# A spectral block and an MLP with all gradients on one core: w1 in column groups, the two MLP weight gradients placed earlier, the last product interleaved with the modulation gradients

## The chip, the core and the metric

The kernel runs on one core of a Trainium2 chip. The metric is the time on the device for one execution, in microseconds, smaller being better. A core has TensorE (PE in the profile, its weight loads PEld), VectorE (DVE), ScalarE (ACT), GpSimd (POOL) and SyncE (SP). Transfers between DRAM and on-chip memory are issued from SP's queue and from POOL's queue; the 16 DMA engines of the core carry both.

## The reference

The forward pass, on x of 2048 tokens by 1024 features in bfloat16, is

```
sa, ca, ga, sb, cb, gb = silu(c) @ w_mod           # six rows of 1024
h = layernorm(x) * (1 + ca) + sa
x = x + ga * irfft2(rfft2(h) * (w_r + 1j * w_i))   # spectral part, A
h = layernorm(x) * (1 + cb) + sb
y = layernorm(h)
x = x + gb * (gelu(y @ w1 + b1) @ w2 + b2)         # MLP, B; hidden width 3584
```

The kernel returns this x and the gradients for A_x, w_r, w_i, w1 (out_4), b1, w2 (out_6), b2, c and w_mod (out_9), given a gradient for the output. B_x is a constant and is not used.

## The kernel before

The program is written as one long sequence on one core. A scheduler of the language orders the instructions of each engine at build time, by the order of the program, the dependences and the memory slots that are free; what it writes down is then fixed, and each engine and each queue runs its list in order, waiting on semaphores. On-chip memory is cut into named regions (tags such as `px0` to `px5`, `sma`, `smb`, `t0` to `t3`, `uv0` to `uv3`, `fr`, `ot`, `wt`, `ph`, `gm`, `sb`): a tile with the tag of an earlier one can be written only when everything that reads the earlier one is done. PSUM has eight banks of 128x512 float32: two with tag `s`, two with `d`, four with `f`. A product of 128x128 by 128x512 is one matmul instruction.

The stages, in the order of the program:

- Modulation rows, matrices of the transforms, the gradient times gb (d_gBo), layernorm and folding of x (lines 169 to 540).
- The spectral forward (`spectral_core`, L342): products with the token transform (`s_fwd`, pu, L337), eight pairs (`pair`: products pcs, L360; complex multiplication with w_r and w_i on DVE, the weights gathered by POOL), products pv (L420), and for each quarter of the tokens products po (L455) and a `consume` function.
- The gradient through w2: `pp` (L575), 896 products, stored to d_ph. It is scheduled into the gaps of the spectral forward.
- The MLP forward with the gradient through the gelu (L601 to L670). `z_block` multiplies one of seven groups of 512 hidden features at a time (32 products pz, L614), then works on ACT and DVE, and stores the hidden values to d_hh and the gradient to d_gz. `bo_pass` multiplies by w2, 112 products pbo (L649) for half of the output columns of a quarter of the tokens, with w2 loaded in seven pieces through three buffers (L645). w1 stays on chip in eight tiles, one for 128 rows each, all 3584 columns wide (L584).
- The MLP backward (L690 to L754): w1 loaded again, transposed, in seven tiles w1T (L696), 896 products pg (L722), then two layernorm gradients (`ln_bwd`) on DVE and ACT, with column sums accS and accC, and the folding into fbuf2.
- The spectral backward, the same `spectral_core` with `consume_bwd` (L773): column sums accCA, `ln_bwd` and out_1. Its o4 tile `ct` has one buffer for the four quarters.
- gw2, the gradient for w2 (L803 to L822): 896 products over 28 row tiles fc. The hidden values come back transposed from d_hh in pieces of 256 features (L812, two buffers), gBo in four tiles gB (L806); the sums are copied by ACT (L821) and stored by POOL to out_6 (L822).
- Column sums accGA, and the gradient for w_mod (L851 to L864): 48 pieces, each loaded (wrw, L860) and reduced by DVE (L863), and made by ACT (gww, L861) and stored by POOL (L862), with four buffers each. "w_mod" in the text is this loop.
- gw1, the gradient for w1 (L876 to L896): 896 products in seven blocks, the gradient transposed from d_gz in 2 MB pieces (L885, two buffers), the sums copied by ACT (L893) and DVE (L895) in turn and stored by POOL (L896).

Though gw2 and gw1 stand at the end of the program, gw2 is started by the scheduler in the gaps of the last quarter products, since its d_hh buffers and gB tiles use memory that is free by then.

## Time and profile before

Three runs took 1913.84, 1921.5 and 1923.69 us; the median is 1921.5. The profiled execution took 1915.37 us, of which its span is 1913.6.

| engine | busy, us | share of the span |
|---|---|---|
| TensorE | 1514.3 | 79% |
| VectorE | 991.2 | 52% |
| ScalarE | 826.9 | 43% |
| GpSimd | 353.2 | 18% |

The two DMA queues moved 347.87 MB, 182 GB/s on the mean. The chain of work that ended last is, by line, issue of instructions (8.8%), the gw2 products (5.8%) and the gw1 products (3.4%), with the rest in many small pieces. A busy share over 1913.6 us is a mean over stages that are bound by different things, so the stages are read one at a time: the busy time of each engine in a stretch, the granted TensorE clock there, the share of time in which the DMA engines were busy (the records overlap a little, so a share can be somewhat over 1), and the waits by who ended them.

### The profile page before, as it was taken

To read this page: it belongs to the slowest core of one execution; us is meant where nothing else is said; L and a number is where in the kernel's file an instruction comes from. 1 tells how busy PE (TensorE), PEld (TensorE's weight loads), DVE (VectorE), ACT (ScalarE), POOL (GpSimd) and SP (SyncE) were. 2 spreads that over 40 slices of the span, in tenths; PEclk is the share of its full clock that TensorE was granted. 3 is DMA by queue.
4 is the path that set the end of the run, shared out by engine and by line. 5 is a ranking of instruction groups with operands and counts; after the bars stand their busy time and mean duration, and the time that the engine had idled before them with its cause. 6 is when DMAs were issued, how large, how long until landed. Compare 5 with 4: busy or idle time off the path is not lost. (4 is left out here: it accounts for less than half of the span.)

```text
span 1913.6 us, 18102 instructions
## 1 busy us (share of the span) xinstructions
PE 1514.3 (79%) x6590; PEld 681.7 (36%) x6722; DVE 991.2 (52%) x1380; ACT 826.9 (43%) x1097; POOL 353.2 (18%) x422
## 2 busy tenths in 40 slices
PE   2328998778988999998688999295479998817998
PEld 1103544333433343443233444042234443303443
DVE  1535556652288667677203787837556660464110
ACT  4636556775566555565011433253333341362000
POOL 5631331111111111111000001015201011132111
PEclk8659998889999999999899999598789999958999
DMA  9994485694365576657993444424636678698551
GB/s 336 254 274 124 125 253 179 175 259 119 111 187 202 198 225 205 203 160 215 202 271 103 165 154 177 131 66 133 176 105 163 160 231 205 214 326 201 125 127 36
DMA packets 396115, 347.87 MB, mean 182 GB/s; under 512 B 245997, under 2 KB 332013, under 8 KB 395898
## 3 DMA queue, kind: packets, MB, share of 16 engines
q1 hardware_dynamic: 361242, 228.17, 45.8%
q0 software_dynamic: 34784, 118.55, 17.8%
q8 instruction: 52, 0.85, 0.2%
q14 instruction: 37, 0.30, 0.0%
HBM read 168.34 MB, written 120.65 MB: 151 GB/s over the span
## 5 line engine op out<-in xcount | busy, mean ns | idle before, releaser
L889 PE MATMUL gw1acc<-gzs,n3n 128*128 128x512 bf16 x879 | 197.1, 385 | 62.1 <-ACT gwo L893 44.6
L575 PE MATMUL pp<-gBoT,wt 128*128 128x512 bf16 x875 | 202.5, 387 | 15.9 <-ACT phr L577 14.8
L722 PE MATMUL pg<-w1T,gzr 128*128 128x512 bf16 x879 | 198.9, 383 | 10.3 <-ACT gn3a L726 5.2
L889 PEld LDWEIGHTS <-n3n 128*128 128x128 bf16 x896 | 88.5, 99 | 170.3 <-issue 67.1
L157 DVE TENSOR_TENSOR ct<-ct 128x2048 bf16<-128x2048 bf16 (+1 forms) x76 | 103.4, 1389 | 60.4 <-ACT ct L457 40.5
L575 PEld LDWEIGHTS <-wt 128*128 128x128 bf16 x896 | 89.7, 100 | 121.9 <-issue 22.2
L614 PEld LDWEIGHTS <-w 128*128 128x128 bf16 x896 | 87.0, 98 | 122.7 <-issue 20.1
L722 PEld LDWEIGHTS <-gzr 128*128 128x128 bf16 x896 | 88.0, 98 | 118.2 <-issue 10.3
L649 PEld LDWEIGHTS <-hhA 128*128 128x128 bf16 x704 | 70.7, 101 | 126.1 <-issue 48.6
L157 DVE TENSOR_TENSOR gt<-gt,gt 128x2048 bf16<-128x2048 bf16 x84 | 102.1, 1224 | 17.9 <-ACT gt L621 17.0
L819 PE MATMUL gw2acc<-gB,hhsA 128*128 128x512 bf16 x438 | 103.3, 393 | 6.1 <-DMA hhsA<-d_hh 5.6
L614 PE MATMUL pz<-n3Tb,w 128*128 128x512 bf16 x439 | 100.3, 381 | 8.1 <-ACT gt L616 7.6
L614 PE MATMUL pz<-n3Ta,w 128*128 128x512 bf16 x438 | 99.2, 379 | 6.1 <-ACT gt L616 5.7
L577 ACT CAST phr<-pp 128x512 bf16<-128x512 f32 x112 | 62.8, 586 | 92.6 <-PE pp L575 58.6
L819 PE MATMUL gw2acc<-gB,otl 128*128 128x512 bf16 x439 | 100.9, 386 | 0.6 <-issue 0.2
L616 ACT ACTIVATE gt<-pz,b_col 128x512 bf16<-128x512 f32 x112 | 74.6, 682 | 50.8 <-PE pz L614 49.5
L895 DVE CAST gwo<-gw1acc 128x512 bf16<-128x512 f32 x28 | 19.3, 691 | 148.6 <-PE gw1acc L889 142.4
L420 PE MATMUL pv<-smi,R 128*128 128x512 bf16 x248 | 60.8, 391 | 40.3 <-DVE R L157 38.1
L893 ACT CAST gwo<-gw1acc 128x512 bf16<-128x512 f32 x28 | 16.3, 584 | 157.1 <-PE gw1acc L889 140.7
L821 ACT CAST gwo<-gw2acc 128x512 bf16<-128x512 f32 x56 | 32.7, 583 | 114.3 <-PE gw2acc L819 106.2
L455 PE MATMUL po<-gm,V 128*128 128x256 bf16 x256 | 45.2, 325 | 45.0 <-ACT ct L457 44.7
L578 POOL DMA_DIRECT2D d_ph<-phr x56 | 40.1, 716 | 210.9 <-ACT phr L577 183.0
(237 smaller groups left out, 2507.5 us busy)
## 6 DMA issues: line engine op xcount, KB each, us to landing
d_ph<-phr POOLq DMA_DIRECT2D x56, 256.0 KB, 3.6
d_gz<-gt POOLq DMA_DIRECT2D x28, 512.0 KB, 5.2
gzr<-d_gz SPq DMA_DIRECT2D x28, 512.0 KB, 7.5
wrw<-in_w_mod_dram SPq DMA_DIRECT2D x48, 256.0 KB, 3.8
out_dram<-gww POOLq DMA_DIRECT2D x48, 256.0 KB, 4.7
d_hh<-hhA POOLq DMA_DIRECT2D x22, 512.0 KB, 4.7
w2sA<-in_B_w_dram SPq DMA_DIRECT2D x19, 512.0 KB, 6.1
w2sB<-in_B_w_dram SPq DMA_DIRECT2D x19, 512.0 KB, 6.2
```

The lines of the kernel that those rows point to most:

```text
L157: nc.vector.tensor_tensor(out=out, in0=a, in1=b, op=op)
L420: nc.tensor.matmul(pv[:], lhsT=R[:, cl * 4 + m, :, :].rearrange("p x w -> p (x w)")[:, base:base + 255:2], rhs=smi[:, cl // 2, m, :], star ...
L455: nc.tensor.matmul(po[:, d2 * 256:(d2 + 1) * 256], lhsT=Vs[cl][:, 2 * dc + h, i * P:(i + 1) * P], rhs=gm[:, gi, :], start=(h == 0), stop=( ...
L575: nc.tensor.matmul(pp[:], lhsT=w2t[:, cch, k * P:(k + 1) * P], rhs=gBoT[b][:, cch, :], start=(cch == 0), stop=(cch == NDC - 1))
L577: nc.scalar.copy(out=ph2[:, k, :], in_=pp[:])
L578: nc.gpsimd.dma_start(out=d_ph_v[:, 2 * fg:2 * fg + 2, b * BW:(b + 1) * BW], in_=ph2)
L614: nc.tensor.matmul(pz[:], lhsT=w1s[cch][:, fc * P:(fc + 1) * P], rhs=n3T[:, cch, :], start=(cch == 0), stop=(cch == NDC - 1))
L616: nc.scalar.activation(out=zb[:, k, :], in_=pz[:], func=ACT.Identity, bias=b1_col[:, fc:fc + 1], scale=1.0)
L649: nc.tensor.matmul(pbs[i][:], lhsT=hh[:, k, i * P:(i + 1) * P], rhs=wp[:, k, :], start=False, stop=(g == 6 and k == 3))
L722: nc.tensor.matmul(pgs[i][:], lhsT=gzt[g][:, k, i * P:(i + 1) * P], rhs=w1Ts[g][:, k, h * KH:(h + 1) * KH], start=(g == 0 and k == 0), sto ...
L819: nc.tensor.matmul(acc[:], lhsT=hhs[:, t, k * P:(k + 1) * P], rhs=gBs[t // 4][:, t % 4, h * KH:(h + 1) * KH], start=(t == 0), stop=(t == N ...
L889: nc.tensor.matmul(acc[:], lhsT=n3ns[t // 4][:, t % 4, cch * P:(cch + 1) * P], rhs=gzs[:, t, :], start=(t == 0), stop=(t == NT - 1))
```

## The change

Five things change.

1. w1 is kept in seven tiles of 512 columns (a group g) by all 1024 rows, loaded one after the other. `z_block` for group g reads tile g alone, so a tile is free for w1T_g as soon as the last quarter's group g is multiplied; w1 and w1T use the same list of tags.
2. The region `px1` is no longer part of w1. Half of it is a fourth buffer for w2, half holds a row of sums `gacc`. The output passes add their column sums there through a PSUM bank each (pa), in place of two banks held throughout (accG); the freed banks (tag `d`) take every second pz.
3. The gB loads, and buffers for d_hh, are placed ahead of the spectral backward in the program. d_hh is now loaded in 28 pieces of 128 features with two buffers in `px1`, which is free at the end of the MLP forward, and two in `ot`. The tile empf moves to `wt`. The banks of accCA are taken, and set to zero by two products with a zero tile, before the spectral backward starts.
4. The last two row tiles of gw2 are summed at once in four banks, one quarter of the tokens after the other.
5. gw1 is split into `gw1_block`s. Block 0 follows gw2; one further block stands behind each of the six rows of w_mod. d_gz is loaded in halves (8 of 16 token tiles) with four buffers.

```
-    W1T = ["sma", "smb"] + PXT
+    W1T = PXT[2:6] + ["sma", "smb", "px0"]
...
-    for cch in range(NDC):
-        wtile = reg.tile([P, F], BF16, name=f"w1_{cch}", tag=W1T[cch])
-        nc.sync.dma_start(out=wtile[:], in_=w1_v[:, cch, :])
+    for g in range(7):
+        wtile = reg.tile([P, NDC, BW], BF16, name=f"w1_{g}", tag=W1T[g])
+        nc.sync.dma_start(out=wtile[:], in_=w1_v[:, :, g * BW:(g + 1) * BW])
...
+    px1t = reg.tile([P, 2, 4, BW], BF16, name="w2sD", tag="px1")
...
+    gacc = px1t[0:1, 1].rearrange("p a b -> p (a b)").bitcast(FP32)
...
-                pz = ps_s("pz")
+                pz = (ps_s, ps_d)[k % 2]("pz")
...
-            wp = w2p[w2n[0] % 3]
+            wp = w2p[w2n[0] % 4]
...
-            nc.tensor.matmul(accG[h][:], lhsT=ones_bf[:], rhs=go[:, i, :], start=(b == 0 and i == 0), stop=(b == 3 and i == 3))
+            nc.tensor.matmul(pa[:], lhsT=ones_bf[:], rhs=go[:, i, :], start=(i == 0), stop=(i == 3))
+        if b == 0:
+            nc.vector.tensor_copy(out=gacc[:, cs_], in_=pa[0:1, :])
+        else:
+            tt(gacc[:, cs_], gacc[:, cs_], pa[0:1, :], ALU.add)
...
+    hhp = reg.tile([P, 2, NT, P], BF16, name="hhsA", tag="px1")
+    gBs = []
+    for b in range(NB):
+        gb_t = reg.tile([P, 4, D], BF16, name=f"gB{b}", tag=PXT[2 + b])
+        nc.sync.dma_start(out=gb_t[:], in_=chunk_rows(d_gBo, b))
...
+    hh_o = [0, 1, 0, 1] + [2, 3, 0, 1] * 6
...
+    accCA = [ps_f("accCA0"), ps_f("accCA1")]
+    for h in range(2):
+        nc.tensor.matmul(accCA[h][:], lhsT=ones_bf[:], rhs=css2[:, 0, 0, 0:512], start=True, stop=False)
...
+    for fc in range(NFC):
+        nc.sync.dma_start_transpose(out=hh_s[hh_o[fc]], in_=d_hh[fc * P:(fc + 1) * P, :])
+        if fc >= NFC - 2:
+            continue
...
+    gzh = [reg.tile([P, 8, 512], BF16, name=f"gzh{k}", tag=PXT[2 + k]) for k in range(4)]
...
+    def gw1_block(fg):
+        gz2 = gzh[2 * (fg % 2):2 * (fg % 2) + 2]
         for k in range(2):
+            nc.sync.dma_start_transpose(out=gz2[k][:], in_=d_gz[fg * 512:(fg + 1) * 512, k * 1024:(k + 1) * 1024])
+        for cch in range(NDC):
+            acc = ps_f("gw1acc")
+            for t in range(NT):
+                nc.tensor.matmul(acc[:], lhsT=n3ns[t // 4][:, t % 4, cch * P:(cch + 1) * P], rhs=gz2[t // 8][:, t % 8, :],
...
+    gw1_block(0)
...
+        gw1_block(1 + ri)
```

The order of the instructions shows what the scheduler made of it. On TensorE at the end of the MLP backward, the rows before are the last column sums (accS and accC, from gn3b and pru) and then the first products pu of the spectral backward:

```order
L722 MATMUL pg<-w1T_5707,gzr_5713 128x512
L167 LDWEIGHTS ones_bf
L167 MATMUL accS_5723<-gn3b,ones_bf 128x512
...
L167 MATMUL accC_5726<-pru,ones_bf 128x512
L337 LDWEIGHTS fbuf_5722
L337 MATMUL pu<-smA_7087,fbuf_5722 128x512
```

and of the change, at the same place:

```order
L786 MATMUL accCA_7117<-cs01b,ones_bf 128x512
L819 LDWEIGHTS hhsA
L819 MATMUL gw2acc<-gB_7096,hhsA 128x512
...
L819 MATMUL gw2acc<-gB_7102,hhsA 128x512
L167 LDWEIGHTS ones_bf
L167 MATMUL accS_5731<-gn3b,ones_bf 128x512
```

The gw2 products now stand between the column sums of the last `ln_bwd` and among the first products pu, 152 of 896 ahead of the first pcs.

On SP behind the MLP backward, before (the loads otl and hhsA are d_hh for gw2, smi is for the spectral inverse, the d_gmod rows store column sums):

```order
L163 DMA d_gmod<-row 1x512
L812 DMA_TRANSPOSE otl<-d_hh 128x16x256
L163 DMA d_gmod<-row 1x512
L812 DMA_TRANSPOSE hhsA<-d_hh 128x16x256
L432 DMA_TRANSPOSE smi<-d_SF 128x4x128
```

and now, two further pieces of d_hh having been issued at the end of the MLP forward:

```order
L163 DMA d_gmod<-row 1x512
L823 DMA_TRANSPOSE hhsA<-d_hh 128x16x128 x2
L163 DMA d_gmod<-row 1x512 x2
L823 DMA_TRANSPOSE hhsA<-d_hh 128x16x128
...
L823 DMA_TRANSPOSE otl<-d_hh 128x16x128 x2
L775 DMA empf<-d_E 128x2048
L398 DMA empf<-d_P 128x2056
L823 DMA_TRANSPOSE hhsA<-d_hh 128x16x128
L432 DMA_TRANSPOSE smi<-d_SF 128x4x128 x16
```

Six more half-size loads stand ahead of the smi loads in place of two, each waiting for its slot.

On ACT in the last stage, before (gwo copies gw1's sums, gww makes the w_mod gradient from gr):

```order
L893 CAST gwo_9680<-gw1acc 128x512
L861 ACTIVATE gww<-gr_9454,u_rt 128x1024 x8
L861 ACTIVATE gww<-gr_9455,u_rt 128x1024 x8
...
L893 CAST gwo_9680<-gw1acc 128x512 x27
```

and now:

```order
L862 CAST gwo_9414<-gw1acc 128x512 x2
L906 ACTIVATE gww<-gr_9645,u_rt 128x1024 x8
L862 CAST gwo_9414<-gw1acc 128x512
L906 ACTIVATE gww<-gr_9646,u_rt 128x1024 x4
...
L906 ACTIVATE gww<-gr_9646,u_rt 128x1024 x3
L862 CAST gwo_9414<-gw1acc 128x512 x14
```

All 48 gww stood between the first and the second copy; now copies stand among them.

On SP, the last d_gx load (for the fourth quarter's `consume_bwd`) now stands behind the load for the third gw1 block, whose buffer block 0 must release:

```order
L854 DMA_TRANSPOSE gzh_9413<-d_gz 128x8x512
L163 DMA d_gmod<-row 1x512
L854 DMA_TRANSPOSE gzh_9410<-d_gz 128x8x512
L806 DMA ct<-d_gx_89 128x4x1024
```

where before it stood ahead of every d_gz load.

More of the change, by code (lines that the diff above doesn't have):

```diff
@@ L785, in consume_bwd @@
         for q in range(4):
[L786 removed]
+            colsum(accCA, tmp[:, q, :], False, i == 3 and q == 3)
         s1c = small.tile([P, 4], FP32, tag="s1c")
@@ new lines @@
+    last = [(fc, h, ps_f("gw2acc")) for fc in (NFC - 2, NFC - 1) for h in range(2)]
+    for b in range(NB):
+        for fc, h, acc in last:
+            for t in range(4 * b, 4 * b + 4):
+                gw2_mm(acc, fc, h, t)
+    for fc, h, acc in last:
+        nc.scalar.copy(out=gwo[:, fc % 2, h * KH:(h + 1) * KH], in_=acc[:])
+        if h == 1:
+            nc.gpsimd.dma_start(out=out_6[fc * P:(fc + 1) * P, :], in_=gwo[:, fc % 2])
+    n3ns = []
+    for b in range(NB):
+        n3n = reg.tile([P, 4, D], BF16, name=f"n3n{b}", tag=f"t{b}")
+        nc.sync.dma_start(out=n3n[:], in_=chunk_rows(d_n3, b))
+        n3ns.append(n3n)
@@ L826 @@
+    gw1_block(0)
+    accGA = [ps_s("accGA0"), ps_s("accGA1")]
     for b in range(NB):
```

86 lines of the change are left out of this document (31 added, 55 removed).

## The prediction

> **What bounds the kernel now.** I read the page's slices first, then the busy time of each engine in the stretches between the program's stages, then the waits of TensorE.
>
> ```profile
> PE   2328998778988999998688999295479998817998
> ```
>
> A slice is 47.8 us. TensorE is the engine that is full wherever nothing is missing; its holes are at the start, in slices 24 to 29 (the end of the MLP backward and the spectral backward) and in slice 35. The stretches (start and end in us; then busy us and instruction count of PE, PEld, DVE, ACT, POOL; granted clock; DMA share; GB/s):
>
> ```profile
> 501.70:890.00 388.30, 356.53 (x1559) 155.19 (x1590) 272.74 (x400) 230.90 (x213) 53.65 (x64) 0.98 0.60 194
> 890.00:977.00 87.00, 60.34 (x244) 24.91 (x246) 29.78 (x47) 16.16 (x17) 5.86 (x7) 0.88 1.11 215
> 977.00:1194.30 217.30, 209.73 (x928) 93.22 (x948) 130.52 (x185) 68.68 (x102) 10.23 (x8) 0.98 0.49 165
> 1194.30:1239.40 45.10, 10.18 (x24) 2.75 (x22) 41.95 (x62) 10.63 (x12) 3.35 (x4) 0.60 0.42 131
> 1239.40:1268.40 29.00, 28.41 (x120) 12.49 (x124) 1.10 (x1) 18.04 (x31) 0.00 (x0) 0.92 0.37 71
> 1268.40:1370.40 102.00, 56.20 (x227) 28.03 (x229) 77.45 (x101) 31.25 (x56) 45.44 (x26) 0.82 0.47 130
> 1370.40:1395.50 25.10, 12.02 (x67) 6.51 (x67) 12.16 (x10) 14.68 (x22) 1.93 (x2) 0.84 0.47 143
> 1395.50:1542.20 146.70, 131.99 (x601) 62.62 (x613) 80.42 (x109) 55.30 (x75) 14.31 (x21) 0.93 0.63 163
> 1542.20:1642.00 99.80, 93.71 (x413) 41.75 (x420) 32.50 (x41) 21.83 (x34) 9.07 (x15) 0.95 0.72 182
> 1656.50:1734.40 77.90, 17.36 (x72) 7.34 (x71) 56.76 (x95) 53.78 (x50) 26.88 (x49) 0.64 0.96 332
> 1734.40:1906.00 171.60, 170.53 (x768) 77.08 (x783) 22.28 (x37) 15.13 (x27) 28.60 (x53) 0.99 0.47 110
> ```
>
> In order: z and output passes; their end with the w1T loads; MLP backward; last ln_bwd; s_fwd; the eight pairs; last pv and first po; the four consumes; the rest of gw2; w_mod; gw1. Length less PE busy gives its idle time: 31.8, 26.7 and 7.6 in the MLP, then 34.9, 0.6, 45.8 and 13.1 (94.4 together) from 1194.3 to 1395.5, 14.7 in the consumes, 6.1, 60.5 in w_mod, 1.1. The waits of TensorE say why:
>
> ```profile
> PE gw1acc L889 <- ACT gwo L893: 44.6, 1, 44.6
> PE gw1acc L889 <- DVE gwo L895: 15.9, 1, 15.9
> PE pbo L649 <- DMA w2sA<-in_B_w_dram: 18.4, 4, 11.5
> PE accCA L167 <- DVE ct L157: 11.8, 2, 11.4
> PE pbo L649 <- DMA w2sC<-in_B_w_dram: 10.0, 3, 5.3
> PE pbo L649 <- DMA w2sB<-in_B_w_dram: 8.1, 3, 3.6
> PE gw2acc L819 <- DMA hhsA<-d_hh: 5.6, 1, 5.6
> ```
>
> The 60.5 us of w_mod (DMA share 0.96) are the first two rows: gw1 has started, and the copies that empty its sums stand on ACT and DVE behind the w_mod loop. In the pairs TensorE has nothing to do while DVE works; gw2 and gw1 need nothing from the spectral stage, but stand behind it.
>
> **What is moved, and what it is worth.** A warm 128x512 product costs 0.216 us: 25.00/116 is 0.2155, 10.74/49 is 0.219.
>
> ```profile
> 1750.00:1775.00 25.00, 24.90 (x116) 11.31 (x117) 2.11 (x4) 2.34 (x4) 3.78 (x7) 1.00 0.71 98
> 1760.30 10.74 PE gw1acc L889 x49
> 1477.73 1.86 PE po L455 x8
> 1461.87 7.23 DMA ct<-d_gx
> ```
>
> Term 1, after the last po. The last product po ends at 1542.2 (with the fourth stretch from the end); from there the kernel takes 1913.6 - 1542.2 = 371.4 us. In the changed order 152 of the 896 gw2 products stand in the last ln_bwd, 117 in the pairs, 91 in the last pv, 50 before the first accCA, 481 among the consumes (about as many as now) and 5 behind the last po. Then follow 896 gw1, 8 accCA, 32 accGA and 2 accSA. Dense, 943 x 0.216 = 203.7 us, and 7.6 from the last product to the end (1913.6 - 1906.0) as now: 211.3, which is 160.1 less. That takes away the 60.5 of w_mod, 85 of gw2 and, with the waits, the products at a low clock (0.64 in the w_mod row).
>
> New stalls are charged against it. First, on SP the third gw1 block's transposed load waits until TensorE has finished the first block, and the last d_gx load is queued behind it; DVE's closing add, gxa multiply and the accGA sums wait for that. About half a gz load on SP (4), the 7.2 of the d_gx row and two DVE operations of 2.3 (timed in the chain fence below) are 16, with 46 products (9.9) ahead of accGA: 6. Second, w_mod now shares the DMA engines. Alone it took 77.9 us at a share of 0.96, 75 us of DMA time. A 2 MB gz load is in these rows:
>
> ```profile
> 1770.00:1780.00 10.00, 9.95 (x47) 4.54 (x47) 0.69 (x1) 1.17 (x2) 1.62 (x3) 1.00 1.03 243
> 1785.00:1790.00 5.00, 5.00 (x25) 2.25 (x24) 0.69 (x1) 0.58 (x1) 0.77 (x2) 1.00 0.07 26
> ```
>
> 10 x (1.03 - 0.07) = 9.6. Some 3.5 of them and the stores of 2.7 blocks (1 MB each, 3 us at the 332 GB/s of the w_mod row) fall into the same time: 75 + 34 + 8 = 117; at 1.11, the share of the 890 to 977 row, 105 us. In DVE's changed order the 48 w_mod reductions stand between ten gw1 copies, that is twenty products' sums, 20 x 16 x 0.216 = 69 us; four PSUM buffers let TensorE run 4 x 16 x 0.216 = 14 ahead. So 105 - 69 - 14 = 22, and with w_mod at its own 77.9 nothing. I take 19, nearer the upper since both must move the same bytes. Together 25; bounds 0 (all hidden) and 60 (w_mod as exposed as now). Term 1: -160.1 + 25 = **-135**.
>
> Term 2, the spectral stage itself. It must carry 360 products more before the first consumes: 77.8 us against 94.4 idle. The cover is thin: 152 x 0.216 = 32.8 in 34.9; 208 x 0.216 = 44.9 in 45.8 of the pairs and what follows; 50 x 0.216 = 10.8 in the accCA wait of 11.4, which is pure cover. Whatever comes late there lies on the chain, since TensorE runs in order and pu, pcs and pv stand behind gw2. In the last ln_bwd the third to fifth d_hh load must wait for a slot; a load is:
>
> ```profile
> L812 SPq DMA_TRANSPOSE hhsA<-d_hh x7: 4591/4939/7877, 1237.7 to 1600.3; - x7
> DMA to landing us min/median/max: 8.3/9.4/10.5
> 1225.84 2.29 DVE L157 TENSOR_TENSOR gn3b<-gn3b,got 128x4096 bf16<-128x4096 bf16 x1
> DVE qb L157 <- DMA empf<-d_P: 12.8, 3, 9.8
> 1286.33 11.09 POOL L351 DMA_INDIRECT ws<-in_A_w_r_dram,xu  x1 [6.61 <-DMA out_dram<-empf]
> ```
>
> Halved loads hold SP some 2.5 us and land in 5 to 9; the fifth, whose tile is released by the DVE operation at 1225.84 (it reads got, of the same memory), then lands at about 1240, where s_fwd starts now, and 24 products (5.2) come after it: +3. In the pairs, loads and gathers already stop DVE (12.8, and one gather of 11.1 on POOL). There are d_hh loads and out_6 stores on the same queues now: I charge one more such gather, +10. In the consumes the count of products is as before and the chain is DVE and DMA, each quarter of it ending with
>
> ```profile
> 1469.19 2.30 DVE ct L157
> 1471.51 5.50 DMA out_dram<-ct
> ```
>
> so +3. Term 2: **+16**, bounds 0 and about 45 (the pairs' products fully on the chain).
>
> On that gather the Trainium skill has a rule that speaks against the change: SBUF — State Buffer, "SBUF: two separate sides", says DVE in a two-port mode locks GpSimd out of the shared port, so that DMAs issued from POOL wait for their descriptors. By it eight stores more on POOL, each behind one 1.23 us operation, would cost 10, and without it the sum would be 10 lower; the 11.09 us row agrees with it, and the stores of the present out_6 group, 0.55 us each, do not:
>
> ```profile
> L157 DVE TENSOR_TENSOR qb<-Pt,empf 128x2052 bf16<-128x2052 bf16 x8 | 9.8, 1227 | 12.8 <-DMA empf<-d_P 12.8
> L822 POOL DMA_DIRECT2D out_dram<-gwo x28 | 15.4, 550 | 194.8 <-ACT gwo L821 194.5
> ```
>
> Term 3, the MLP.
>
> ```profile
> L696 SPq DMA_TRANSPOSE w1T<-in_B_w_dram x28: 1226/2106/7446, 891.6 to 971.0; - x28
> L585 SPq DMA_DIRECT2D w<-in_B_w_dram x8: 328/328/519, 254.1 to 284.9; - x8
> L614 PE MATMUL pz<-n3Ta,w x438: 375/379/380, 425.0 to 783.0; 128*128 128x512 bf16 x146
> ```
>
> With w1 in eight row tiles no w1T tile can be loaded until the last pz; all 28 transposes then run into the w2 loads (share 1.11), and TensorE is idle for 26.7 us from 890 to 977. With column groups, four of the seven go in one output pass earlier, and there are four w2 buffers in place of three. The last three groups still come at the end of z, on SP ahead of the next w2 load: I leave 7 of the 26.7, so -20. For the four PSUM banks of pz I credit nothing: the 31.8 idle of z is spread over 388 us. The copy of the pa sum, eight small ones on DVE (busy 272.74 of 388.30), lies beside 112 products. The 1 KB pieces of w1 cost nothing: w1 is issued by 285, and the first pz is at 425. Term 3: **-20**, bounds -36.5 (all three pbo rows) and +10 (transposes in the way of d_ph loads).
>
> Sum against the profiled execution: 1915.4 (span 1913.6 and 1.8 around it) - 135 + 16 - 20 = 1776. This execution is 6.1 below the median of the runs shown, 1921.5; I add half: **1779 us**. Its own range is 1752 to 1808.
>
> **Rivals.** One of them needs this row:
>
> ```profile
> L806 SPq DMA_DIRECT2D gB<-d_gBo x4: 372/448/460, 1174.7 to 1190.4; - x4
> ```
>
> Clean cover: neither w_mod nor the spectral chain notices the other work. Without the 25 and the 16: 1738. For it: w_mod and gw1 have no data in common. Against: both use SP in order.
>
> The end is bound by DMA: w_mod and the gz loads follow each other, and term 1 takes its 60: 1779 + 35 = 1814. For it: 75 + 7 x 9.6 + 7 x 3 for the stores is 163 of 204 us, and the gz loads stand on SP between runs of 16 w_mod loads.
>
> The first gw2 products come late, because gB and the first d_hh loads meet the loads of the next stage: the 32.8 of the last ln_bwd stay behind: 1812. For it: the gB loads are four of 1 MB in the last 20 us of the MLP; against: they are issued there now too.
>
> Short rows: d_hh lands in rows of 256 bytes, before 512. If a piece costs the same whatever its size, three exposed loads take 4.7 longer each: 1793. Against it, rows of this trace:
>
> ```profile
> 1254.50:1279.00 24.50, 24.45 (x114) 12.81 (x114) 6.25 (x10) 16.39 (x28) 2.41 (x2) 1.00 0.40 84
> 1228.00:1238.00 10.00, 0.00 (x0) 0.00 (x0) 9.90 (x9) 0.00 (x0) 0.80 (x1) 0.50 0.89 210
> ```
>
> 256-byte rows (smi): 9.8 us of DMA time for 2.06 MB; 512-byte rows (d_hh, with a store) 8.9 for 2.1.
> The Trainium skill (DMA: Bandwidth & Descriptors, "Specifications") states that rule: below 512 bytes a read-modify-write. These rows do not bear it out for transposes.
>
> Slower than before: 24 of the 28 d_hh loads wait at the head of SP for TensorE to free a slot, the spectral loads stand behind them, and TensorE's next gw2 product waits for the load. If each exposes its 9.4, 24 x 9.4 = 226: 1779 + 226 = 2005. From the fifteenth exposure on (139/9.4) it is slower. Against: now one such wait shows, 5.6 us.
>
> That the work does not move at all, 1915, is nearly excluded by the order.
>
> **How the numbers follow.** Forecast 0.64, clean cover 0.11, DMA-bound end 0.13, late start 0.05, short rows 0.03, slower 0.03, nothing 0.01. The range 1738 to 1830 reaches from the clean cover to term 1 at its upper bound (+35) together with term 2 doubled (+16). About 0.5% is what a measurement of this kernel can tell from no change: faster 0.96, within 0.01, slower 0.03.
>
> **What would show it.** Right: no wait of gw1acc above 15 us; PE busy over 85% from 1194 on; the last po some 4 us earlier or later than 1542; from it to the end 230 to 245; waits of pbo under 15 in all. Wrong: pv or pu waiting for d_hh; DVE's reductions spread over more than 110 us with gw1acc waiting for its copies; a longer z stage, where I claim only the tail.

## The result and the profile after

The changed kernel takes 1783.1 us (median of four runs, 1767.1 to 1788.1) against 1922.6 us for the kernel before (four runs, 1913.8 to 1924.3). The ratio is 0.927, with a 95% interval of 0.920 to 0.934. The forecast was 1779 us. The sum is right to 4 us (and 9 above the profiled execution: 1776 against 1767.1), but in these profiles two of its three terms are wrong by 30 us and more, in opposite directions, and most of what follows is on these two. The profiled execution of the changed kernel took 1767.1 us (span 1765.2), 148.4 less in span than the one before.

The slices of the page of the changed kernel, in tenths of busy time; a slice is 44.1 us:

```profile
PE   3328998678998989999979999989889887986598
DMA  9995468567447666679994244763675567899991
```

TensorE's hole in the spectral stage (slices 24 to 29 before) is filled. One is left in slices 36 to 38, 1545 to 1677 us, where the DMA engines are full: gw1 and w_mod run side by side there.

Busy time by stretch, changed kernel (start and end in us; length; then busy us and instruction count of PE, PEld, DVE, ACT, POOL; granted clock; DMA share; GB/s). In order: first to last pz; to the first pg; the MLP backward; the spectral stage to the last po; from there to the end; the part of that with w_mod's reductions in it; the gw1 products that follow.

```profile
419.80:859.40 439.60, 416.32 (x1868) 185.84 (x1905) 288.07 (x428) 271.66 (x281) 69.39 (x84) 0.99 0.68 207
859.40:926.70 67.30, 54.33 (x232) 23.37 (x237) 25.42 (x43) 14.29 (x13) 5.88 (x7) 0.92 1.05 265
926.70:1138.20 211.50, 209.25 (x929) 93.30 (x948) 133.29 (x187) 69.17 (x105) 8.24 (x9) 0.99 0.45 144
1138.20:1498.40 360.20, 316.04 (x1417) 150.12 (x1446) 210.41 (x281) 142.33 (x217) 72.61 (x63) 0.95 0.60 161
1498.40:1765.20 266.80, 214.11 (x926) 94.23 (x942) 121.56 (x183) 76.67 (x88) 58.89 (x107) 0.93 0.86 214
1555.70:1680.00 124.30, 84.72 (x341) 36.08 (x347) 64.63 (x108) 55.60 (x58) 36.88 (x69) 0.86 1.07 282
1679.60:1757.20 77.60, 76.60 (x348) 34.80 (x355) 10.25 (x19) 6.45 (x11) 12.99 (x24) 1.00 0.60 94
```

The same stretches of the kernel before, cut at its own products; the last row is its end, from the last po:

```profile
425.00:893.10 468.10, 428.68 (x1870) 186.90 (x1907) 286.73 (x426) 272.36 (x281) 67.16 (x84) 0.97 0.57 182
893.10:977.20 84.10, 57.29 (x230) 23.69 (x235) 26.68 (x41) 14.84 (x14) 5.86 (x7) 0.88 1.15 223
977.20:1194.70 217.50, 210.06 (x929) 93.26 (x949) 130.92 (x185) 68.92 (x103) 10.63 (x8) 0.98 0.49 166
1542.20:1913.60 371.40, 294.62 (x1308) 131.81 (x1332) 121.45 (x182) 93.22 (x112) 65.64 (x119) 0.90 0.65 179
```

To the last pg the change gains 56 us (1194.7 - 1138.2), the spectral stage costs 13 more (360.3 against 347.5), and the end gains 105 (371.4 - 266.8).

Rows of the waits in the end of the changed kernel (engine, line, waited for; us in total, times, longest):

```profile
ACT gwo L862 <- PE gw1acc L858: 84.2, 12, 10.9
DVE wrw L908 <- DMA wrw<-in_w_mod_dram: 60.7, 20, 16.6
ACT gww L906 <- DMA out_dram<-gww: 40.2, 14, 10.4
PE gw1acc L858 <- ACT gwo L862: 31.6, 6, 13.2
ACT gwo L862 <- DMA out_dram<-gwo: 22.6, 4, 10.5
DVE gwo L864 <- DMA out_dram<-gwo: 12.4, 1, 12.4
```

TensorE waits for the copies of its sums, the copies stand behind w_mod's instructions, and those wait for DMAs. The longest of these waits can be followed through three engines. TensorE:

```profile
1630.09 7.07 PE L858 MATMUL gw1acc<-gzh,n3n 128*128 128x512 bf16 x31 [1.55 <-ACT gwo L862]
1650.38 9.91 PE L858 MATMUL gw1acc<-gzh,n3n 128*128 128x512 bf16 x32 [13.22 <-ACT gwo L862]
```

ACT, which copies a sum at 1629.5 and the next at 1649.8, with six products of w_mod between them, five of which waited for an earlier store (four of the rows):

```profile
1629.48 0.57 ACT L862 CAST gwo<-gw1acc 128x512 bf16<-128x512 f32 x1
...
1643.32 1.15 ACT L906 ACTIVATE gww<-gr,u_rt 128x1024 bf16<-128x1024 f32 x1 [3.77 <-DMA out_dram<-gww]
1648.71 1.15 ACT L906 ACTIVATE gww<-gr,u_rt 128x1024 bf16<-128x1024 f32 x1 [4.24 <-DMA out_dram<-gww]
1649.76 0.57 ACT L862 CAST gwo<-gw1acc 128x512 bf16<-128x512 f32 x1
```

SP, where the two halves of a gz load are under way all that time, 23.4 us for what took 7.4 to 8.5 in the kernel before:

```profile
1629.71 23.42 SPq L854 DMA_TRANSPOSE gzh<-d_gz  x2
```

### The profile page after: what moved, and what is told of

It is laid out like the page before. It is cut to its first block, busy times and chain, and to the rows that moved or that the text cites. A ratio compares the mean times of both kernels' runs of the same rounds, so it can differ in the third digit from the quotient of the medians.

```text
span 1765.2 us, 18125 instructions
## 1 busy us (share of the span) xinstructions
PE 1498.5 (85%) x6591; PEld 681.0 (39%) x6724; DVE 991.9 (56%) x1386; ACT 822.0 (47%) x1097; POOL 355.5 (20%) x422
## 5 line engine op out<-in xcount | busy, mean ns | idle before, releaser
L858 PE MATMUL gw1acc<-gzh,n3n 128*128 128x512 bf16 x877 | 203.7, 391 | 42.4 <-ACT gwo L862 31.6
L819 PE MATMUL gw2acc<-gB,hhsA 128*128 128x512 bf16 x501 | 119.0, 389 | 1.9 <-ACT gwo L831 1.0
L819 PE MATMUL gw2acc<-gB,otl 128*128 128x512 bf16 x374 | 94.3, 405 | 9.2 <-DMA otl<-d_hh 5.4
L908 DVE CUSTOM_DVE_ANT_0 wrw<-wrw,gr 128x1024 bf16<-128x1024 bf16 x48 | 56.9, 1221 | 60.8 <-DMA wrw<-in_w_mod_dram 60.7
L906 ACT ACTIVATE gww<-gr,u_rt 128x1024 bf16<-128x1024 f32 x48 | 52.4, 1141 | 58.8 <-DMA out_dram<-gww 40.2
L819 PEld LDWEIGHTS <-hhsA 128*128 128x128 bf16 x512 | 51.7, 101 | 63.8 <-issue 8.7
```

The lines of the kernel that those rows point to most:

```text
L819: nc.tensor.matmul(acc[:], lhsT=hh_s[hh_o[fc]][:, t, :], rhs=gBs[t // 4][:, t % 4, h * KH:(h + 1) * KH], start=(t == 0), stop=(t == NT - 1))
L858: nc.tensor.matmul(acc[:], lhsT=n3ns[t // 4][:, t % 4, cch * P:(cch + 1) * P], rhs=gz2[t // 8][:, t % 8, :], start=(t == 0), stop=(t == NT ...
L906: nc.scalar.activation(out=gw, in_=grep_, func=ACT.Copy, scale=u_rt[:, jc:jc + 1])
L908: nc.vector.tensor_tensor_reduce(out=wr, in0=wr, in1=gbf, scale=1.0, scalar=0.0, op0=ALU.mult, op1=ALU.add, accum_out=gu[:, r, jc:jc + 1])
```

## The experiments

Twelve kernels ran. Their stage lengths, in us, from TensorE's timeline of the profiled execution of each; the median and the ratio to the kernel before on the same chip come from the timed runs.

| kernel | first pz to last pg | last pg to last po | last po to end | median | ratio (95%) |
|---|---|---|---|---|---|
| before | 769.7 | 347.6 | 371.4 | 1922.6 | |
| changed | 718.4 | 360.4 | 266.7 | 1783.1 | 0.927 (0.920 to 0.934) |
| groups_alone | 738.7 | 345.6 | 376.2 | 1895.7 | 0.986 (0.980 to 0.992) |
| pz_two_banks | 736.7 | 358.4 | 257.6 | 1784.2 | 0.931 (0.923 to 0.938) |
| w2_three | 729.1 | 356.5 | 262.7 | 1774.8 | 0.924 (0.916 to 0.931) |
| gw2_late | 726.9 | 349.4 | 337.1 | 1837.6 | 0.959 (0.950 to 0.967) |
| no_wmod_bytes | 718.2 | 354.4 | 215.7 | 1722.6 | 0.898 (0.893 to 0.903) |
| wmod_last | 719.0 | 357.2 | 286.7 | 1795.6 | 0.937 (0.931 to 0.943) |
| paced | 729.9 | 362.9 | 267.9 | 1790.2 | 0.934 (0.928 to 0.940) |
| accga_early | 722.0 | 362.1 | 270.2 | 1795.3 | 0.936 (0.928 to 0.944) |
| copies_on_act | 720.9 | 357.3 | 248.4 | 1758.2 | 0.918 (0.914 to 0.922) |
| copies_on_act_pool_stores | 722.0 | 355.9 | 267.0 | 1774.5 | 0.927 (0.923 to 0.931) |
| sixteen_copy_buffers | 720.3 | 355.4 | 258.9 | 1770.4 | 0.926 (0.918 to 0.933) |
| copies_on_act_sixteen | 723.2 | 359.8 | 249.8 | 1758.4 | 0.915 (0.911 to 0.919) |

How far a single profile can be trusted is in the table too. Ten runs have the changed kernel's MLP unaltered; theirs is 718.2 to 729.9. The end, where it is unaltered (changed, pz_two_banks, w2_three), is 257.6 to 266.7, and the changed kernel's own is the longest of the three. The first pz comes anywhere from 419.8 to 441.7, so the 5 us by which it came earlier after the change are not the change's.

### The MLP: which part gave 51 us

groups_alone is the kernel before with w1 in column groups:

```
-    W1T = ["sma", "smb"] + PXT
+    W1T = PXT[2:6] + ["sma", "smb", "px0"]
...
+    for g in range(7):
+        wtile = reg.tile([P, NDC, BW], BF16, name=f"w1_{g}", tag=W1T[g])
```

> The kernel before, with only w1 kept in seven column groups, whose tiles the w1T groups then take over in the same order; three w2 buffers, two PSUM banks for pz, accG and everything behind the MLP stay. The changed kernel's MLP was 56 us shorter (8 before z, 25 within z and the output passes, 17 between the last pz and the first pg, 6 in the backward). Theory groups: the tail's 17 and the 8 ahead of z belong to them: 20 to 30 us faster than before, about 1895. Theory that the groups bring all of it: 45 to 56 faster, about 1870. Theory that the fourth w2 buffer and the two more banks bring it: within 10 us of before.

It is 1.4% faster than before (0.8 to 2.0%), some 27 us. The same three stretches (columns as above):

```profile
433.90:897.60 463.70, 427.70 (x1908) 186.04 (x1907) 286.74 (x426) 271.79 (x280) 67.33 (x83) 0.98 0.65 197
897.60:963.70 66.10, 53.48 (x235) 23.12 (x236) 24.33 (x39) 14.33 (x13) 5.86 (x7) 0.90 1.05 260
963.70:1172.50 208.80, 207.52 (x949) 92.52 (x948) 133.19 (x187) 69.51 (x104) 8.22 (x9) 1.00 0.44 145
```

The groups give 18 us at the tail (66.1 against 84.1), 9 in the backward (208.8 against 217.5) and 4 within z: 31 of the 51. The 4 are within the scatter of z, which is 438.8 to 448.7 in the ten unaltered runs. Of the 9, 5.2 are one wait that the trace of the kernel before shows and that of groups_alone does not: TensorE waits for a copy of its sums on ACT (gn3a, L726), and that copy stands behind an instruction that waits 6.2 us for the load of gm. What is left is in z.

pz_two_banks and w2_three each take one other part of the change back:

```
-                pz = (ps_s, ps_d)[k % 2]("pz")
+                pz = ps_s("pz")
```

```
-            wp = w2p[w2n[0] % 4]
+            wp = w2p[w2n[0] % 3]
```

> The changed kernel, with the sums pz of z in two PSUM banks in turn, as in the kernel before, in place of four; the column groups and the four w2 buffers stay. The column groups alone left the z part (first pz to last pz 463.7 us, before 468.1) as it was and took 18 us from the time between the last pz and the first pg and 8 from the backward; the changed kernel's z part is 439.6. Theory banks: with two banks z goes back to 460 to 468, the time rises by 18 to 28, to about 1805; waits of pz for ACT come back to about 12. Theory w2: the z part is short because of the fourth w2 buffer; then this run is within 6 us of the changed kernel, about 1783.

> The changed kernel, with three w2 buffers in turn in place of four; four banks for pz stay. Theory banks: within 8 us of the changed kernel (1783), z part about 440 to 448, waits of pbo for w2 up from 10 to 20 or so. Theory w2: z part back to 460 or more, the time above 1800.

With two banks z takes 456.7 us in place of 439.6, and the wait for ACT that the kernel before had comes back. Waits of pz in the run with two banks, and in the kernel before:

```profile
PE pz L616 <- ACT gt L618: 12.9, 14, 3.0
```

```profile
PE pz L614 <- ACT gt L616: 13.2, 13, 3.1
```

In the changed kernel it is 3.5. The MLP as a whole is 14.6 longer than the mean of the ten unaltered ones (736.7 - 722.1), outside their scatter. TensorE's waits in it are 47.1 us in all, against 33.8 to 40.5 in the ten; and TensorE is busy in z for 426.2 us where the changed kernel has 416.3, at a granted clock of 0.98 against 0.99.

With three w2 buffers the MLP is 7 longer (729.1), still inside the scatter. The waits tell more than the length. These are the rows of that run for w2:

```profile
PE pbo L651 <- DMA w2sA<-in_B_w_dram: 17.6, 4, 11.2
PE pbo L651 <- DMA w2sC<-in_B_w_dram: 9.6, 4, 4.9
PE pbo L651 <- DMA w2sB<-in_B_w_dram: 2.6, 4, 0.9
```

That is 29.8 us, where the ten unaltered runs have 10.4 to 17.3; but other waits of the stage became shorter, so that all of TensorE's waits in it are 42.7, 6 above the mean of the ten. So the banks are worth some 15 us in this stage; the fourth w2 buffer takes waits for w2 away, but of that the stage shows only 7 us, inside its scatter. The total did not show either: expected was 1805 with two banks, measured 1784, since the end of that run happened to be 9 us shorter and a ratio has an interval of 1.5%. The stage shows what the total can't.

### The spectral stage: what the early gw2 costs and brings

gw2_late puts the first gw2 tile into memory that is free only behind the pairs. The line moves from ahead of the spectral stage to behind it:

```
-    hhp = reg.tile([P, 2, NT, P], BF16, name="hhsA", tag="px1")
...
+    hhp = reg.tile([P, 2, NT, P], BF16, name="hhsA", tag="px0")
```

> The changed kernel, with the first gw2 tile in memory that is free only after the eight pairs, so that gw2 starts behind them: 556 gw2 products in place of 891 are done at the last po, 335 (72.4 us) go behind it. Theory term 2 (the early gw2 products cost the spectral stage 12): last pg to last po falls from 360 to 346 to 350. For the stretch from the last po to the end, now 266.8: theory products, dense work sets it and the 55 of stalls stay: 339, the time 1783 - 12 + 72 = about 1843. Theory traffic: the stalls belong to bytes that must move anyway, and 72 us of products that need few bytes give them room: 285 to 300, the time about 1795 to 1805, so that the early gw2 as it stands is worth only 15 to 20 us.

From the last pg to the last po it takes 349.4, as without the change (347.6 and 345.6); the eleven runs with early gw2 products take 354.4 to 362.9, 358.2 in the mean. The early products cost the chain about 11 us. In return the end is 70.4 us longer without them (337.1 - 266.7; 74 and 80 against the two shorter unaltered ends), for 335 products that are 72.4 us dense. The gain of this part of the change is thus about 60 us, and 61 by the ratios of the two kernels. The theory that w_mod would make use of the longer end failed: it did not run there. TensorE goes through gw2 at full speed, and reductions of w_mod begin only at 1624.9, behind it.

```profile
1525.00:1550.00 25.00, 25.00 (x117) 11.31 (x116) 10.81 (x17) 6.35 (x9) 4.21 (x6) 1.00 0.69 180
1550.00:1575.00 25.00, 25.00 (x117) 11.35 (x116) 0.00 (x0) 3.66 (x7) 1.20 (x3) 1.00 0.57 140
...
1650.00:1675.00 25.00, 11.85 (x54) 5.18 (x53) 12.96 (x23) 10.25 (x10) 6.54 (x13) 0.83 1.17 227
1675.00:1700.00 25.00, 15.18 (x58) 6.27 (x58) 10.39 (x18) 10.48 (x11) 6.75 (x13) 0.69 1.04 305
```

So the run doesn't say what w_mod beside gw2 would give. That was not tried.

### The end: whose are the 55 us

Of the 266.8 us in the end 211 are dense products and the tail; 55 are stalls, where 25 were predicted. By the other two unaltered ends it would be 46 and 51. no_wmod_bytes leaves the loads and stores of five rows of w_mod out:

```
-            nc.sync.dma_start(out=wr, in_=w_mod[jc * P:(jc + 1) * P, r * D:(r + 1) * D])
+            if ri == 0:
+                nc.sync.dma_start(out=wr, in_=w_mod[jc * P:(jc + 1) * P, r * D:(r + 1) * D])
...
-            nc.gpsimd.dma_start(out=out_9[jc * P:(jc + 1) * P, r * D:(r + 1) * D], in_=gw)
+            if ri == 0:
+                nc.gpsimd.dma_start(out=out_9[jc * P:(jc + 1) * P, r * D:(r + 1) * D], in_=gw)
```

> The changed kernel, with the loads and stores of five of w_mod's six rows left out (so most of out_9 is not written and gu is not the reference's); their ACT products and DVE reductions stay. From the last po the changed kernel took 266.8 us, of which 211 are dense products and the tail, so 55 are stalls. Theory traffic: the stalls come from w_mod's bytes on the DMA engines; the stretch falls to 215 to 230, the time to about 1725. Theory instructions: the 48 products of 1.1 us on ACT and 48 reductions of 1.2 us on DVE hold the copies of gw1's sums; the stretch stays above 250, the time above 1750.

The end and, below it, that of wmod_last, which puts w_mod behind gw1:

```profile
1499.40:1715.00 215.60, 204.98 (x943) 91.92 (x941) 120.38 (x183) 75.00 (x88) 37.20 (x67) 1.00 0.67 167
```

```profile
1507.00:1793.60 286.60, 204.50 (x943) 91.94 (x941) 122.77 (x183) 78.34 (x88) 58.95 (x107) 0.87 0.69 199
```

Without the bytes the stalls are gone: 215.6, within 4.3 of the dense sum (211.3), at a clock of 1.00, though ACT and DVE carry out every instruction they did (75.0 and 120.4 us busy, 76.7 and 121.6 in the changed kernel). The instructions of w_mod hold nothing up by their own time; its transfers do. Leaving them out takes away their time on the DMA engines and also the waits of ACT, DVE and the queues for them, so this run does not tell these two apart. The edit of wmod_last, whose first two lines stand ahead of the loop over w_mod's rows:

```
+    for fg in range(1, 7):
+        gw1_block(fg)
...
-    wrw = reg.tile([P, 4, D], BF16, name="wrw", tag="uv2")
-    gww = reg.tile([P, 4, D], BF16, name="gww", tag="uv3")
+    wrw = reg.tile([P, 4, D], BF16, name="wrw", tag="px4")
+    gww = reg.tile([P, 4, D], BF16, name="gww", tag="px5")
...
-        gw1_block(1 + ri)
```

> The changed kernel, with w_mod put behind gw1: its load and product buffers take the memory of the gz tiles of the sixth block, so that no row of w_mod starts before that block's products. This gives up the interleaving. Theory traffic (gw1 alone has no stalls): gw1 dense, its last product at about 1498 + 206 = 1704, then w_mod's 78 us less what lies beside the last block (up to 20): 1765 to 1790 in all, so that the interleaving as it is in the changed kernel is worth only 0 to 20 us. Theory that gw1's own transposed loads and stores cause part of the 55: the last gw1 product comes later than 1720 and the time is above 1790. Theory that the interleaving saves most of w_mod: above 1820.

With w_mod last, gw1 is dense to its last product at 1715.9, and w_mod follows, its reductions from 1689.7 to 1775.9: 1795.6 us, 6 more than the traffic theory allowed. The interleaving, as it stands, saves 12 of 1783 by the medians, whose ratios have intervals that overlap, and 20 by the ends of the two profiles (286.7 - 266.7; 29 against the shortest unaltered end), of the 75 that w_mod would cost in full (286.7 - 211.3).

The share of DMA time says why the rest is not to be had cheaply. Length by share gives the DMA engines' time in the end: 286.6 x 0.69 = 198 us where w_mod and gw1 don't overlap, 266.8 x 0.86 = 229 where they do. TensorE's dense work is 204. So neither leaves much room in 211 us, and side by side the packets take 31 us longer. The size of that surplus is not a constant: the other runs that move the same bytes side by side have 218 us (copies_on_act) to 235 (copies_on_act_pool_stores).

paced was to test whether w_mod is only taken too fast (its reductions span 124 us of the end; gw1 has 204). Each piece shares a slot with the copy of one gw1 column, so that it can't run further ahead than eight columns. A slot holds the piece of w_mod and the product, and later the copy:

```
+    slots = [prs[k // 2][:, k % 2] for k in range(8)]
...
+            sl = slots[(fg * NDC + cch) % 8]
+            if piece is not None:
+                piece(cch, sl)
-            ob = gwo1[:, (fg * NDC + cch) % 4]
+            ob = sl[:, :, 0:256]
```

> The changed kernel, with w_mod's 48 pieces paced by gw1's columns from its first block on: a piece's load, its product and the sum of one gw1 column share one of eight slots, so that piece n+8 waits for the store of column n. All bytes and all arithmetic stay. Theory bunching: the stalls come from taking all of w_mod beside only twenty columns; spread over 48 columns (166 us of products) the DMA engines are not overfull, the stretch from the last po to the end falls from 267 to 220 to 235, the time to 1720 to 1740. Theory that the bytes decide wherever they lie (gz loads, stores and w_mod are 105 + 88 us of DMA time in 204): the stretch stays at 255 or more, the time at 1755 or more. A slower result (above 1785) would mean that the chain load, reduction, product, store, copy in one slot has become the limit.

> The paced kernel (w_mod's pieces in eight slots shared with gw1's columns), with the gx1 and A loads and accGA moved from behind the first gw1 block to behind the pairs, where they need no result of the spectral stage, into memory that is free there; the slots take the memory that accGA had. In the paced run TensorE lost 43 us between 1500 and 1600, 16 of them in accGA, whose loads stood on SP behind w_mod loads that waited for slots; from 1600 to 1750 it lost 12 at a DMA share of 0.85. Theory order on SP: that loss goes to 15 or less, the stretch from the last po to the end is 225 to 240, the time 1740 to 1755 (below the changed kernel). Theory bytes: w_mod, gz loads and stores need the engines wherever the waits stand; the stretch stays at 255 or more, the time at 1770 or more.

accga_early is paced with accGA and its loads moved to directly behind the spectral stage's call, in other memory:

```
-        gxa = reg.tile([P, 4, D], BF16, name="gxa", tag=f"uv{2 * (b % 2)}")
+        gxa = reg.tile([P, 4, D], BF16, name="gxa", tag=("sma", "wt")[b % 2])
```

In both, the theory that promised a shorter end fails. The reductions are spread over 220 us (1524.1 to 1743.7 in paced), and the end is 267.9 and 270.2. Nothing is won, and by the medians both kernels are a little slower than the changed one (the intervals overlap). The waits in the end of accga_early:

```profile
DVE pr L902 <- DMA pr<-in_w_mod_dram: 111.9, 28, 11.3
ACT pr L900 <- DMA out_dram<-pr: 93.7, 24, 11.8
PE gw1acc L873 <- ACT pr L878: 32.1, 13, 7.2
PE gw1acc L873 <- DMA gzh<-d_gz: 9.9, 2, 7.9
```

The two waits for DMAs are about twice those of the changed kernel: a paced piece still waits, in front of the copies. In part that may be the slot itself, which ties load, product, store and copy into a chain: paced took 1790.2 us, above the 1785 that its expectation named as the sign of that chain. Also, these two kernels store gw1 in rows of 512 bytes where the changed one has 1 KB; how much each of these costs was not measured.

copies_on_act parts the two kinds of work by engine. All copies of gw1 and their stores go to ACT, w_mod's products to DVE:

```
-            if cch % 2 == 0:
-                nc.scalar.copy(out=ob, in_=acc[:])
-            else:
-                nc.vector.tensor_copy(out=ob, in_=acc[:])
-            nc.gpsimd.dma_start(out=out_4[cch * P:(cch + 1) * P, fg * 512:(fg + 1) * 512], in_=ob)
+            nc.scalar.copy(out=ob, in_=acc[:])
+            nc.scalar.dma_start(out=out_4[cch * P:(cch + 1) * P, fg * 512:(fg + 1) * 512], in_=ob)
...
-            nc.scalar.activation(out=gw, in_=grep_, func=ACT.Copy, scale=u_rt[:, jc:jc + 1])
+            nc.vector.tensor_scalar(out=gw, in0=grep_, scalar1=u_rt[:, jc:jc + 1], scalar2=None, op0=ALU.mult)
```

copies_on_act_pool_stores is the same with the stores of out_4 left on nc.gpsimd.

> The changed kernel with the work of w_mod and of gw1 parted by engine: all 56 copies of gw1's sums and the stores behind them go to ACT and its own queue, and w_mod's 48 products go from ACT to DVE, beside its reductions; w_mod's loads stay on SP and its stores on POOL. Bytes, arithmetic and TensorE's order stay. The paced runs had the DMA engines below full (share 0.85) and still 55 us of stalls, while ACT waited 51 to 94 us for w_mod's stores and DVE 82 to 112 for its loads, with the copies in order behind these instructions. Theory shared queues: the stalls come from copies behind w_mod instructions that wait for a DMA; parted, the stretch from the last po to the end is 215 to 235 (dense 211) and the time 1735 to 1755. Theory bytes: the stretch stays at 255 or more, the time at 1770 or more; gw1's sums then wait for its own stores or gz loads.

> As the run with all copies on ACT and w_mod's products on DVE, but the stores of gw1 stay on POOL's queue, in order with w_mod's stores. Theory queue of the engines: what matters is that the copies do not stand behind w_mod instructions on ACT and DVE; within 6 us of the run with the stores on ACT. Theory POOL's queue: a gw1 store behind a w_mod store that waits for its product holds the four copy buffers; of the stalls taken away by the other run, more than half (20 us or more) come back, as waits of ACT's copies for gw1's stores. Theory bytes: 255 or more from the last po to the end in both.

With the stores on ACT the end is 248.4, 18 less than in the changed kernel and 9 less than the shortest of the three unaltered ends; the time is 1758.2. With the stores on POOL, behind w_mod's, nothing is won (267.0). ACT has no other work then, and yet its copies wait:

```profile
ACT gwo L861 <- DMA out_dram<-gwo: 128.7, 24, 17.3
PE gw1acc L858 <- ACT gwo L861: 29.7, 4, 14.2
```

So the queue that holds the stores matters more than the engine that holds the copies (the stores on ACT's queue with the copies left on both engines were not tried). But copies_on_act is not the 215 to 235 that was expected either. Its waits:

```profile
ACT gwo L861 <- DMA wrw<-in_w_mod_dram: 59.4, 10, 12.5
PE gw1acc L858 <- ACT gwo L861: 27.3, 6, 13.2
ACT gwo L861 <- DMA gzh<-d_gz: 16.2, 1, 16.2
```

The last two runs give the copies sixteen buffers in place of four, in the changed kernel and in copies_on_act:

```
-    gwo1 = reg.tile([P, 4, 512], BF16, name="gwo1", tag="ph")
+    gwd = [reg.tile([P, 8, 512], BF16, name=f"gwo1{t}", tag=f"sm{t}") for t in "ab"]
+    gwo1 = [gwd[k // 8][:, k % 8] for k in range(16)]
```

> The changed kernel with sixteen buffers for the copies of gw1's sums in place of four, in memory that is free after the last pv; nothing else. Theory copy buffers: in the changed kernel copies of gw1's sums wait for their own stores (22.6 us on ACT, 12.4 on DVE), since a 128 KB store lands late while a transposed gz load and w_mod hold the DMA engines; with sixteen buffers the stretch from the last po to the end falls from 267 to 240 or less, the time to 1755 or less. Theory shared queues: the copies still stand on ACT and DVE behind w_mod instructions that wait for DMAs (40 us on ACT, 61 on DVE), so the stretch stays at 255 or more.

> The run with all copies and gw1's stores on ACT and w_mod's products on DVE (stretch from the last po to the end 248.6, 27.3 us of waits of TensorE for ACT's copies, in two groups while a gz load of 10 to 11 us ran), with sixteen copy buffers in place of four. Theory: what was left there is copies waiting for late stores; with sixteen buffers the waits for copies go below 5 us, the stretch to 220 to 230, the time to about 1738. Theory bytes: the gz loads themselves come later, the waits of TensorE move from the copies to gz, and the stretch stays above 242.

sixteen_copy_buffers has an end of 258.9, within the scatter of the unaltered ones. The waits of copies for their own stores are gone from its list, and TensorE waits for the copies nearly as long as before (14.3 + 14.3 on ACT, 31.6 in the changed kernel): the shared queue was left. copies_on_act_sixteen has 249.8, no better than with four. Its waits for copies are 30.8, not below 5:

```profile
PE gw1acc L859 <- ACT gwo1a L862: 18.3, 2, 16.4
PE gw1acc L859 <- ACT gwo1b L862: 12.5, 2, 7.7
```

The longest of them in ACT's timeline; ACTq are the stores it issues:

```profile
1680.52 0.58 ACT L862 CAST gwo1a<-gw1acc 128x512 bf16<-128x512 f32 x1 [7.01 <-DMA wrw<-in_w_mod_dram]
1700.18 0.34 ACTq L863 DMA_DIRECT2D out_dram<-gwo1a  x1
1700.57 0.59 ACT L862 CAST gwo1a<-gw1acc 128x512 bf16<-128x512 f32 x1 [19.46 <-DMA gzh<-d_gz]
1701.18 0.34 ACTq L863 DMA_DIRECT2D out_dram<-gwo1a  x1
```

The copy was done at 1681.1, its store was issued at 1700.2, and the next copies followed at once. What held ACT was the issue of a store, not a full buffer. The instruction list of this program names what such a store waits for:

```
712 L863 DMA out_dram<-gwo1a 128x512 [waits DMAHW3_49,Activation_49]
714 L863 DMA out_dram<-gwo1a 128x512 [waits DMAHW4_49,Activation_49]
```

Besides ACT itself it is one of eight completion counters, DMAHW0 to DMAHW7, which SP's loads of w_mod and gz wait for in the same way. A store on ACT can thus wait for an earlier load of SP with which it shares a counter and no data. In the program that this kernel builds, 28 of the 56 stores wait for a counter value that a transfer issued by SP brings. The store issued at 1700.18 is the 35th; its counter is DMAHW0, at the value that a load of gz brings, which is the releaser that the trace names. All four waits of TensorE for the copies gwo1a and gwo1b in this run (30.8 us) end in the same way, with a copy right behind such a store: the other three stores, issued at 1617.18, 1639.57 and 1653.47, wait for loads of w_mod. This is read from the program and the trace; a kernel that changes the counters was not tried, and how early those loads could land is not known either.

By the medians copies_on_act and copies_on_act_sixteen (1758) are 25 us faster than the changed kernel, by the ratios 17 and 22; the interval of the second (0.911 to 0.919) lies wholly below the changed kernel's (0.920 to 0.934), the first overlaps it at the edge.

## Why the prediction came out as it did

**Term 1, the end: -105 measured, -135 predicted.** The dense sum was right: 211.3, and 215.6 with most of w_mod's bytes left out. The step that failed is the charge for new stalls, 25 (6 + 19), which measured 55 (46 to 55 over the three unaltered ends). Of the 6 for accGA, 2.0 came, as waits for gxa. The 19 rested on 117 us of DMA time at a share of 1.11, that is 105 us of w_mod. The reductions took 124 us, at a share of 1.07, 133 us of DMA time. Put into the same formula, 124 - 69 - 14 = 41, it would have given 47 in all. That is near, but paced speaks against the formula as the mechanism: there w_mod was spread over 220 us, the formula gives nothing, and the stalls stayed, though paced also has the chain through its slots. What does stand is the count behind the rival of a DMA-bound end. It put 163 us of DMA time beside 204 us of products; the whole end has 198 with gw1 and w_mod apart and 229 with them together. The loads of gx1, A and gx and of the rows gr, and the stores of the last quarter, were left out of the 163. The rival's price (60 us of stalls) was nearly met, and the forecast gave it 0.13. The stalls come from w_mod's transfers (shown by leaving them out). That the copies are held through queues and the issue of stores is shown in part, by the 9 to 18 us that copies_on_act wins; of the 38 us left in copies_on_act_sixteen, 31 are waits for copies behind a store that waits for a load of SP. How much of these is the shared counter and how much the load of the DMA engines stays open.

**Term 2, the spectral stage: +13 measured, +16 predicted.** From the last pg to the last pu it is 79.3 against 73.7, from there to the last pv 112.9 against 109.6, from there to the last po 168.1 against 164.1: 5.6, 3.3 and 4.0, where 3, 10 and 3 stood. gw2_late, with 349.4, shows that the early gw2 products are the cause. The fifth d_hh load came late as described:

```profile
PE gw2acc L819 <- DMA otl<-d_hh: 5.4, 1, 5.4
```

The 10 in the pairs was too much: DVE's waits there for loads (empf and pf from d_P) are 20.0 us, against 16.1 before and 15.1 in gw2_late, which is about the 3.3. The waits for DVE's R, which were TensorE's hole, went from 36.0 to 7.8 (the stage's waits of pv), as foreseen; the cover held, and a second slow gather did not come. POOL's gathers in the pairs of the changed kernel:

```profile
L351 POOL DMA_INDIRECT ws<-in_A_w_r_dram,xu x6: 986/1723/11122, 1225.4 to 1290.0; - x6
L832 POOL DMA_DIRECT2D out_dram<-gwo x6 | 3.6, 593 | 9.8 <-ACT gwo L831 9.8
```

There is one of 11.1, as before, and the six out_6 stores that now stand among them take 0.59 each, five of them while an operation of DVE ran. The Trainium skill's rule on the port that DVE and GpSimd share (SBUF — State Buffer, "SBUF: two separate sides") was weighed at 10 us there; these rows show no such delay for a store from POOL beside a busy DVE. In which mode DVE ran then, no row shows.

**Term 3, the MLP: -51 measured, or -56 with the scatter ahead of it; -20 predicted.** This lies outside the bounds that the prediction gave (-36.5 and +10). The tail, the one thing that was credited, gave 17 (84.1 to 67.3; 18 in groups_alone). Three things were left out. The backward became 6 to 9 us shorter, which groups_alone shows to belong to the groups; the wait of 5.2 us behind the load of gm is gone in both kernels. z became 4 shorter with the groups, which the scatter could account for too. And the four PSUM banks, credited with nothing since "the 31.8 idle of z is spread over 388 us", are worth about 15: the waits view of before has the row for it, 13.2 us in 13 waits of pz for ACT, and the prediction read only the sum of the stretch. Thirteen waits of 1 us with one cause are one term, however spread they are. A sum of waits is not all of it either: of the 28.5 us by which z became shorter, 16.1 are idle time and 12.4 are the same products at a granted clock of 0.99 in place of 0.97 (busy for 428.7 and 416.3 us).

**The signs that were named.** No wait of gw1acc above 15 us: right (13.2). PE busy over 85% from 1194 on: 483.7 of 571.2 us, 84.7%, a near miss. The last po within some 4 us of 1542: wrong, 1498, since the MLP was shorter. From it to the end 230 to 245: wrong, 267. pbo's waits under 15: 15.6, a near miss. The sign against it, reductions over more than 110 us with gw1acc waiting for copies, came: 124.

The total was right by luck: term 1 gained 30 us less than forecast and term 3 gained 31 to 36 more, and with 3 from term 2 these cancelled. The range held for the same reason.

## What to carry to other kernels

Before work is laid side by side, add up the DMA time of all that will share the stretch, stores and small loads of its neighbours too, and compare it with the dense time of the engine that is to hide it: 198 against 204 us left little room here, and pacing and deeper buffers moved the waits about without taking them away. Copies that empty an accumulator should not stand on an engine or a DMA queue behind instructions that wait for loads of something else; parting both gave 9 to 18 us here, and parting the engines without the queue gave nothing. And read the waits by their cause, not by the stretch: a short wait that comes back thirteen times is worth one more bank.

## What the runs showed of the hardware

A transposed load takes longer beside w_mod's plain loads and stores. Half a gz load held SP for 3.8 us at its fastest and 12.9 at its slowest in the changed kernel:

```profile
L854 SPq DMA_TRANSPOSE gzh<-d_gz x14: 3776/7586/12942, 1480.4 to 1709.0; - x14
```

Without w_mod beside it, in wmod_last, the median is 5.0:

```profile
L854 SPq DMA_TRANSPOSE gzh<-d_gz x14: 3812/5044/9470, 1487.9 to 1664.0; - x14
```

The DMA engines' time for the same bytes went from 198 to 229 us when they were moved side by side (218 to 235 in the other such runs), and in gw2_late the share of a stretch of 25 us went to 1.19 while its rate fell to 191 GB/s, against 332 where w_mod ran alone in the kernel before.

TensorE's clock followed the stalls: 0.86 in the stretch with w_mod, 1.00 in the dense one behind it. Ten of the 55 us are products at the lower clock (214.1 us busy for what is 203.7 at 0.216 each).
